# Hedgehog attention and maxout FFN on one core: q and k of all 16 units loaded as bf16 from GpSimd's queue, side by side in the transposed tile

## The chip, the cores and the metric

The kernel runs on one core of one Trainium2 chip. The metric is the device time of one execution in microseconds (us). A profile of one execution stands beside it. In its rows PE is TensorE, PEld its weight loads, DVE VectorE, ACT ScalarE, POOL GpSimd and SP SyncE; a q behind a name (POOLq, SPq) is that engine's sequencer, which issues transfers and waits on semaphores. L565 is line 565 of the kernel.

## The reference

```python
def phi(x):                                    # x: [8, 8, 576, 64]; w_phi: [64, 128]
    proj = np.einsum('bhsd,df->bhsf', x, w_phi)
    proj = proj - np.max(np.abs(proj), axis=-1, keepdims=True)
    return np.concatenate([np.exp(proj), np.exp(-proj)], axis=-1)
q_p, k_p = phi(q), phi(k)
kv  = np.einsum('bhsf,bhsd->bhfd', k_p, v)
z   = np.sum(k_p, axis=2)
num = np.einsum('bhsf,bhfd->bhsd', q_p, kv)
den = np.einsum('bhsf,bhf->bhs', q_p, z)[..., None] + 1e-06
x   = (num / den)                              # -> [4608 tokens, 512]
h   = np.maximum(np.maximum(x @ w1, x @ w2), x @ w3)   # w1, w2, w3: [512, 768]
out = h @ w_out                                        # w_out: [768, 512]
```

The row maximum of `phi` is taken out of the exponent: the kernel makes exp(p) and exp(-p) without it and puts the factors exp(-m) and exp(m) on v (for k) and on the quotient (for q).

## The kernel before, in words

**Units and chunks.** The attention is cut into 16 units of 4 heads, two units per batch element. A unit has 18 tiles of 128 rows of q and 18 of k: 16 main tiles of q (the first 512 positions of each head) and two tiles of "tails" (the last 64 positions of the four heads). The FFN is cut into nine chunks of 512 tokens: chunk b takes the main tokens of units 2b and 2b+1, the ninth the tails of all of them.

**A unit** runs through these steps (line numbers of the profile):

- Loads. Units 0 to 3 (`by_pe`) load q and k as bf16 into `qk_bf` by transfers that GpSimd issues (L450, L465), except that k of unit 0 comes as float32 by SP (L457) and is cast by DVE (L461). Units 4 to 15 load q and k as float32 into `q_raw` and `k_raw` by SP's queue, and GpSimd casts them into `qk_bf` in four or five pieces per unit (L509). The tails of q come by SP in two small transfers for two units. v comes by SP as float32 into `v_raw`; the loads of v of units 1, 2 and 3 wait for a one-element copy on DVE (`gate`, L478).
- Transposition to `qkT`. Units 0 to 3: TensorE transposes into the PSUM tile `tps` (L494), DVE copies out (L499). Units 4 to 15: one DMA transpose from SP's queue (L513). A tile of q lies above the k tile of the same number (rows 0 to 63 and 64 to 127 of one column block; the other way round from tile 8 on).
- Projections "G" (L535): for each tile one 64-row product for q (`psq`) and one for k (`psk`), in two halves of the array at a time. ACT makes exp(p) and exp(-p) of k (`Ek`, L544), DVE the absolute row maxima (`mk`, `mq`, L547).
- ACT makes the factors `em` (L557); GpSimd multiplies v with them (`vab`, L565) and appends the factors (L569). TensorE sums "K" (L586, `kvps`), 72 products per unit.
- The projections of q the other way round "M" (L606, `psm`), their exponentials `Eq` on ACT (L612), the products "N" with `kv_sb` (L637, `psn`), the sum, reciprocal and quotient (DVE L640 to L645, GpSimd L647 into `x_sb`), and the transposition into `xT` (TensorE and copies for units 0 to 5, a DMA transpose on SP for the rest).

**FFN.** max(x@w1, x@w2, x@w3) is computed from differences: w2 - w1 and w3 - w1 are formed in `w_bf` on GpSimd and DVE (L762), one matmul per difference follows (`ups`, L687), evacuated with a maximum (L693 to L697), and the part through w1 is put into the output as one product with w1@w_out. That product is made once, from a transposed w1 (L774) and w_out (L788). The output products are L715 and L720, the evacuation L728, the stores L735. The four weight loads are issued by GpSimd (L420). A chunk's products need `xT` of its two units and the differences.

**What sets the order.** Every step is a `Node`. The string `PLAN` lists all nodes in the order of their issue, with the engine (T is TensorE, D DVE, A ACT, G GpSimd, S SP), the numbers of the buffers, and after the @ a due time; the nodes are emitted in this order, and each engine works through its own share of it strictly in order, waiting at an instruction whose operand isn't ready. A transfer that GpSimd issues is an instruction in GpSimd's order like any other: its waits hold up what stands behind it. Transfers of one queue take turns on eight semaphores; the ninth issue on a queue waits until the first has landed, the tenth until the second, and so on.

Of the kernel before, what the change touches and what calls it, by code (L numbers as in the profile page):

```python
# [16 lines left out]
DF = 128  # L17
DM = H * D
# [12 lines left out]
GROUPS = [(0, 4), (4, 4), (8, 4), (12, 4), (16, 2)]  # L31
BATCHES = [(0, 8), (8, 8), (16, 2)]
# [7 lines left out]
JOIN = 2  # L40
MOVE = 5
VA_DVE = 1
QK = 3
# [41 lines left out]
8S0@0.7 5G0@1.2 6S@1.3 2S@1.9 4G@2.1 10S0@3.1 9D@3.5 11S0@4.4 7D@4.5 0G@5.0 3D@5.3 92G1@5.6 15T0@6.0 93G@6.4 16D0@6.7  # L85
177G2@7.3 29T000100@7.4 34T23@7.7 31A@7.9 33D@7.9 13T4@8.0 37D@8.5 30A@8.5 12G@8.9 14D@9.1 176G@9.2 36A@9.3 17T0@9.3
38D@9.7 24T45@9.9 35A@9.9 96G@10.0 19T67@10.1 18D@10.3 26A@10.4 178S0@10.4 32D@10.6 39T03@10.7 68T200@10.8 21A@10.9
42D@11.2 25A@11.4 43D@11.5 40A@11.8 22D@11.9 58T10@12.0 48A0@12.1 41A@12.3 27D@12.5 51G0@12.5 20A@12.6 99T3@13.0
28D@13.1 69A@13.1 44A@13.4 63T75@13.6 61A@13.6 23D@13.7 47G@13.7 97T4@13.9 1173G@13.9 65A@14.1 100D1@14.3 101T6@14.4
59A@14.5 50G@14.7 102D@14.9 70A@15.0 98D@15.1 118T013611@15.3 60A@15.3 94D@15.7 64A@15.8 46G@15.8 122D@15.8  # L90
152T411@15.9 95S@16.0 103T12@16.0 120A@16.3 106D@16.5 184T3@16.7 62A@16.8 49G@16.9 107D@17.1 182T7@17.1 104A@17.2
121D@17.7 154A@17.7 113T01@17.8 105A@18.0 45G@18.1 185D0@18.3 153A@18.5 71A0@18.8 183D@18.9 55T024@18.9 67A@19.0
252G1@19.2 114A@19.5 117D@19.5 52T37@19.7 56A@19.9 253G@20.0 57A@20.1 116D@20.1 66A@20.2 108T20@20.3 54A@20.7
112D@20.8 1176G@20.9 147T45@20.9 115A@20.9 111D@21.4 53A@21.4 123T72@21.5 119A@21.5 1174G@21.7 72T31@21.7 127D@22.0
125A@22.0 1187T6@22.2 151A@22.3 73D0@22.3 181G@22.5 126D@22.7 128A0@22.8 80T73@22.9 149A@23.0 74D@23.1 131G0@23.1
109A@23.5 1188D0@23.5 129G@23.5 1185T1@23.7 124A@24.0 81D1@24.1 148A@24.2 83T62@24.4 179D1@24.5 130G@24.6 82D@24.7
150A@24.7 186T7@24.8 1183T4@25.0 84D@25.1 110A@25.2 187D@25.5 75T53@25.6 132A@25.7 85D@25.8 1186A@25.9 133G@26.0
142T06@26.0 76D@26.2 136T072@26.3 86D0@26.6 1184D@26.8 143A@26.8 228T500@26.9 257T1@27.1 256G@27.2 137A@27.3 77D@27.4
87G0@27.4 138A@27.4 329S0@27.5 261T4@27.6 144A@27.6 206T007200@27.8 262D1@27.9 229A@28.1 210D@28.2 159T34@28.3
155A0@28.4 258D@28.5 230A@28.6 134G@28.6 156T07@28.7 400S@28.8 208A@28.8 90T5@29.0 78D0@29.1 146A@29.1 157D1@29.3  # L100
1193T1@29.3 327S@29.4 160D@29.7 135G@29.7 145A@29.8 1175G@29.9 328S0@30.0 158D@30.1 91A@30.2 161D@30.5 401S@30.7
197T3076@30.7 79G@30.7 1194A@30.9 209D@30.9 139T45@31.2 180S@31.3 162D1@31.3 198A@31.4 201D@31.4 1191T1@31.9
163G1@31.9 141A@32.0 200D@32.0 202A@32.2 140A@32.6 205D@32.7 207A@32.8 199A@33.1 167T34@33.2 1178G@33.2 204D@33.3
164T72@33.5 1192A@33.6 168D1@33.9 223T05@33.9 203A@34.1 259T1@34.2 165D@34.3 226A@34.5 169D@34.7 218T36@34.8 224A@35.0
88T7@35.1 166D@35.1 1195T4@35.4 227A@35.5 254D@35.5 170D1@35.7 255S@35.8 1179D@35.8 219A@36.0 89D@36.5 171G@36.5
221A@36.5 172T5@36.7 260D@36.9 220A@37.0 1189T27@37.0 225A@37.5 1D@37.5 1177D@37.7 222A@37.9 174T3@38.3 1181G@38.3
173D@38.3 1196A@38.4 188T6701@38.7 175D@38.9 1190A@38.9 293T4511@39.2 192D@39.4 1205T3@39.5 297A@39.6 190A@40.1
1201T6@40.4 1182D@40.4 193A@40.6 1180D@41.0 1206A0@41.1 1217T2@41.2 194A@41.6 191D@41.7 403G1@41.7 1202A@42.1
1213T3@42.1 405G@42.2 196D@42.3 331G2@42.5 294A@42.6 1218D@42.9 1207T6@43.0 404G@43.0 296A@43.1 1214D@43.5 189A@43.6
333G@43.6 1209T0@43.8 1208A@44.1 195D@44.1 332G@44.2 295A@44.6 281T117511@44.8 407G@44.9 272T1632@44.9 473S0@45.0  # L110
211A0@45.1 284D@45.2 1210A@45.3 1203T4@45.5 334G@45.5 543S@45.6 276D@45.6 277A@45.8 212G0@46.2 285D@46.2 475S@46.2
282A@46.3 1199T0@46.3 279D@46.6 1204A@46.6 283A@47.1 275D@47.2 1219T7@47.2 1200A@47.5 335S0@47.5 280D@47.8 278A@48.0
263T0154@48.2 213G@48.3 1220D@48.4 214A@48.4 274A@48.6 1211T2@48.7 270D@49.0 265A@49.1 273A@49.5 1215T7@49.6 266D@49.7
268A@50.0 267D@50.3 406G@50.4 286A1@50.5 215T063@50.6 231A0@50.7 1212D@50.9 269A@50.9 288G1@51.0 264A@51.4 1216D@51.5
303T2@51.8 298T40@51.9 216A@52.0 217D@52.1 1221T1@52.2 304A@52.3 271D@52.5 301A@52.6 287G@53.0 305A@53.1 240T36@53.1
544S0@53.3 1222D@53.3 302A@53.3 243T57@53.4 1231T2@53.7 289A@53.8 474S@53.9 241D1@53.9 299A@53.9 244D@54.4 408S1@54.5
300A@54.6 232T31@54.6 242D@54.8 235T50@54.9 306A1@55.1 477G0@55.1 245D@55.2 290T146@55.4 233D0@55.6 478G@55.7
236D@56.0 546G2@56.4 246D1@56.5 366T3700@56.6 292A@56.8 291D@56.8 1232T@56.9 547G@56.9 367A@57.1 237D@57.1 548G@57.5
234D@57.6 369A@57.6 247G1@57.8 368A@58.0 238D0@58.1 318T64@58.2 1233D0@58.4 370A@58.5 371T51@58.6 315T03@58.9
239G@59.0 374A@59.1 319D1@59.1 1223T2@59.2 316D@59.5 375A@59.7 320D@60.0 330S1@60.0 310T06@60.1 373A@60.2 479G@60.2  # L120
317D@60.4 248T1@60.4 476S0@60.7 307T47@60.8 549G@60.8 321D0@61.0 249A@61.0 1224T@61.1 311D0@61.1 683S0@61.3 322G0@61.3
308D@61.5 372A@61.6 613S@61.9 312D@61.9 309D@62.4 250T4@62.4 1225A1@62.6 409T11536111@62.8 313D1@62.9 251D@63.1
314G@63.2 439T7011@63.2 411A@63.5 413D@63.5 325T2@63.6 1227T4@63.9 415A@64.0 412D@64.1 1197G@64.4 440A@64.5 326D@64.7
323T5@64.7 443A@65.0 1228T@65.1 416D@65.2 410A@65.4 550G@65.5 324D@65.8 442A@65.9 417D@66.2 551S2@66.3 1247T5@66.4
441A@66.4 686G1@66.7 1229D2@66.8 414A@66.9 687G@67.3 336T00076300@67.3 1248A1@67.5 376T1@67.8 480G@67.9 427T24@67.9
344D@68.0 1235T5@68.1 377A@68.1 428A@68.4 431D@68.6 341A@68.7 339D@69.0 1236T@69.0 429A@69.2 342A@69.5 430D@69.6
337A@69.9 340D@70.0 615S@70.0 1243T4@70.3 378A@70.4 1237D3@70.6 338A@70.7 343D@71.2 345T2610@71.3 684S0@71.3
1244A@71.4 354T75@71.7 402S@71.9 1245T3@71.9 346A@72.0 352D@72.0 355A@72.5 614S@72.5 349D@72.6 347A@72.7 1255T4@72.8
688G@72.9 617G2@73.1 481S0@73.1 351A@73.2 348D@73.4 618G@73.7 1253T2@73.7 356A@73.7 353D@74.0 1246A@74.0 350A@74.5
1241T6@74.5 358D@74.6 690G@74.7 357D@74.9 1256D@75.3 1259T7@75.4 359A1@75.4 1242A@75.7 360G1@75.8 379A1@76.2  # L130
1254D@76.3 418T3450@76.4 1239T6@76.9 422D@77.1 423A@77.1 362A@77.6 421D@77.7 1251T1@77.8 361G@77.8 425D@78.3 419A@78.4
1261T3@78.7 1240D@78.9 420A@79.1 1260D@79.5 1249T2@79.5 424A@79.6 1234S@79.6 619G@79.9 432A0@80.0 426D@80.1 753S0@80.2
# [159 lines left out]
def kernel(  # L292
# [58 lines left out]

    raws = {}
    loaded = {}

    def raw_bufs(u):
        if u // 2 not in raws:
            raws[u // 2] = [buf(f"{x}_raw", 2 if x == "v" else 1, [P, 2 * UT, D], FP32) for x in "qkv"]
        return raws[u // 2]  # L360
# [494 lines left out]
```

## Time and profile before

| | |
|---|---|
| median of 3 runs | 291.16 us (290.9 to 291.44) |
| the profiled execution: its own time | 292.95 us |
| its span, from the first to the last instruction | 291.2 us |
| TensorE busy | 268.1 us, 92% of the span |
| DVE, ACT, GpSimd busy | 237.7, 190.7, 163.5 us |
| mean granted TensorE clock | 0.991 |
| read from HBM, written to HBM | 34.67 MB, 9.44 MB |

A row of the chain of waits in order of time has the start, the duration and what ran (or what was waited for). A row of the timeline has the start, the duration of the merged instructions, the engine, the line, the operation and the count, and in brackets the idle time before it with what ended that. A row of busy time by stretch has the stretch, its length, then for PE, PEld, DVE, ACT and POOL the busy time and the number of instructions, then the granted clock of TensorE, the share of the 16 DMA engines (it can exceed 1, since packets of two queues overlap on one engine) and GB/s.

### The profile page before, as it was taken

Reading aid. Unit: us, or ns where it says so; the run is one execution under the profiler, and the core shown is the slowest. Engines: PE = TensorE matmul, PEld = TensorE weight load, DVE = VectorE, ACT = ScalarE, POOL = GpSimd, SP = SyncE. Lnnn points to the kernel's source line nnn. Section 1 sums busy time; section 2 is a strip of 40 time slices with the busy share of each in tenths; the row PEclk is TensorE's granted clock in tenths of the full one; section 3 lists DMA queues with packets and bytes.
Section 4 is the critical chain, followed back from the end, with each engine's and each line's share of the span. In section 5 each row is a group of like instructions: output and inputs, shape, how many; then the busy total and the mean of one; then the engine's idle time right before and its main releaser. Section 6 shows DMA issues by size and latency. Waiting matters only on the chain.

```text
span 291.2 us, 8530 instructions
## 1 busy us (share of the span) xinstructions
PE 268.1 (92%) x3457; PEld 151.1 (52%) x3502; DVE 237.7 (82%) x474; ACT 190.7 (65%) x471; POOL 163.5 (56%) x169
## 2 busy tenths in 40 slices
PE   1898896998999899999999999998999999999993
PEld 1566552465546454664565455664454664444442
DVE  2889887898899789988999999988989895674641
ACT  1799894987986699589963899898969820000000
POOL 6297859798479787795495536855526373000000
PEclk9999997999999999999999999999999999999998
DMA  8989994999799999999997427993504105200054
GB/s 160 228 175 187 253 287 195 196 254 300 160 297 260 204 356 203 211 283 217 282 244 196 136 46 184 227 138 100 156 2 118 73 2 128 108 0 2 0 161 129
DMA packets 70664, 49.94 MB, mean 172 GB/s; under 512 B 47072, under 2 KB 58720, under 8 KB 70624
## 3 DMA queue, kind: packets, MB, share of 16 engines
q1 hardware_dynamic: 65232, 44.25, 61.8%
q0 software_dynamic: 5312, 5.08, 11.1%
q8 instruction: 27, 0.44, 0.6%
q14 instruction: 13, 0.11, 0.1%
q10 hardware_dynamic: 80, 0.07, 0.1%
HBM read 34.67 MB, written 9.44 MB: 151 GB/s over the span
## 4 chain that ended last, share of the span: by engine, by line
PE 74%; DMA 10%; POOL 4%; issue 4%; ACT 4%; DVE 3%; POOLq 0%; DVEq 0%
PE ups L687 31%; PE ops L720 13%; PE ops L715 9%; PE kvps L586 6%; PE psn L637 5%; DMA w_bf<-in_moe_w_dram 5%; PE psq L535 5%; PE psm L606 3%; ACT Ek L544 2%; DMA xT<-x_sb 2%; POOL w_bf L762 2%; DMA qk_bf<-in_q_dram 2%; PE tps L494 2%; POOL vab L565 1%; POOL x_sb L647 1%
## 5 line engine op out<-in xcount | busy, mean ns | idle before, releaser
L687 PE MATMUL ups<-xT,w_bf 128*128 128x512 bf16 x410 | 100.4, 384 | 4.8 <-POOL w_bf L762 2.6
L544 ACT ACTIVATE Ek<-psk 128x512 bf16<-128x512 f32 (+1 forms) x160 | 84.2, 576 | 16.3 <-PE psk L535 11.9
L612 ACT ACTIVATE Eq<-psm 128x512 bf16<-128x512 f32 (+1 forms) x160 | 82.7, 583 | 12.7 <-PE psm L606 10.8
L565 POOL TENSOR_TENSOR vab<-v_raw,em 128x1152 bf16<-128x1152 f32 (+1 forms) x36 | 67.8, 1907 | 22.6 <-ACT em L557 19.9
L687 PEld LDWEIGHTS <-w_bf 128*128 128x128 bf16 x432 | 40.1, 99 | 52.5 <-issue 5.6
L547 DVE TENSOR_REDUCE mk<-psk 128x4 f32<-128x512 f32 (+1 forms) x80 | 49.5, 630 | 4.8 <-PE psk L535 3.6
L647 POOL TENSOR_TENSOR x_sb<-y,rden 128x640 bf16<-128x640 f32 x32 | 40.4, 1270 | 19.0 <-DVE rden L645 12.1
L720 PE MATMUL ops<-wout_bf,hT 128*128 128x512 bf16 (+1 forms) x214 | 50.0, 373 | 0.7 <-issue 0.5
L547 DVE TENSOR_REDUCE mq<-psq 128x4 f32<-128x512 f32 (+1 forms) x80 | 48.4, 627 | 2.1 <-PE psk L535 2.1
L693 DVE TENSOR_TENSOR hT<-hT,ups 128x512 bf16<-128x512 bf16 x54 | 36.2, 678 | 8.1 <-PE ups L687 7.2
L728 ACT COPY osb<-ops 128x512 f32<-128x512 f32 (+1 forms) x11 | 6.4, 578 | 53.9 <-PE ops L720 53.9
L640 DVE TENSOR_TENSOR y<-psn,sq 128x325 f32<-128x325 f32 x64 | 29.3, 487 | 4.2 <-PE psn L637 4.1
L720 PEld LDWEIGHTS <-hT 128*128 128x128 bf16 x222 | 20.6, 98 | 22.5 <-issue 1.1
L643 DVE TENSOR_TENSOR y<-y,psn 128x325 f32<-128x325 f32 x64 | 29.6, 486 | 1.2
L637 PEld LDWEIGHTS <-Eq 128*128 128x128 bf16 x640 | 24.8, 97 | 9.5 <-issue 2.4
L637 PE MATMUL psn<-kv_sb,Eq 128*128 128x65 bf16 x640 | 26.9, 194 | 1.2 <-issue 1.0
L728 DVE COPY osb<-ops 128x512 f32<-128x512 f32 (+1 forms) x26 | 17.5, 677 | 12.7 <-PE ops L720 11.8
L535 PE MATMUL psq<-wph,qkT 64*128 64x128 bf16 x288 | 25.0, 225 | 1.4 <-DVE qkT L499 1.2
L535 PEld LDWEIGHTS <-qkT 64*128 64x128 bf16 x576 | 18.5, 97 | 14.2 <-issue 10.3
L535 PE MATMUL psk<-wph,qkT 64*128 64x128 bf16 x288 | 24.5, 225 | 0.3 <-DVE qkT L499 0.2
L715 PE MATMUL ops<-xT 128*128 128x512 bf16 x86 | 24.0, 380 | 0.7 <-issue 0.2
L586 PE MATMUL kvps<-vab,Ek 64*128 64x65 bf16 x1152 | 22.3, 191 | 1.5 <-issue 1.1
(57 smaller groups left out, 260.8 us busy)
## 6 DMA issues: line engine op xcount, KB each, us to landing
v_raw<-in_v_dram SPq DMA_DIRECT2D x16, 576.0 KB, 5.9
out_dram<-osb SPq DMA_DIRECT2D x32, 256.0 KB, 3.0
k_raw<-in_k_dram SPq DMA_DIRECT2D x12, 576.0 KB, 5.6
q_raw<-in_q_dram SPq DMA_DIRECT2D x12, 512.0 KB, 6.1
w_bf<-in_moe_w_dram POOLq DMA_DIRECT2D x3, 768.0 KB, 12.5
q_raw<-in_q_dram SPq DMA_DIRECT2D x16, 64.0 KB, 5.5
qk_bf<-in_k_dram POOLq DMA_DIRECT2D x3, 288.0 KB, 8.0
qk_bf<-in_q_dram POOLq DMA_DIRECT2D x3, 256.0 KB, 5.7
```

The costliest lines, as they stand in the source:

```text
L535: nc.tensor.matmul(ps()[:, i, :], lhsT=cols[r0:r0 + D, :], rhs=wph[r0:r0 + D, :], start=True, stop=True)
L544: "ek", {"ACT": 0.485 if n == 4 else 0.28}, lambda s=s, t0=t0, n=n, psk=psk: nc.scalar.activation(Ek[s]()[:, t0:t0 + n, :], psk()[:, 0:n, ...
L547: reds.append(nd(kind, {"DVE": 0.607 if n == 4 else 0.34}, lambda ps=ps, m=m, t0=t0, n=n: nc.vector.tensor_reduce(m()[:, t0:t0 + n], ps()[ ...
L565: made.append(any_of(n_, lambda n_, g=g, t0=t0, t1=t1: (nc.vector if n_.eng == "DVE" else nc.gpsimd).tensor_tensor(vab()[:, g, t0:t1, 0:D] ...
L586: nc.tensor.matmul(kvps[ab]()[:, pr, g, :], lhsT=Ek[g]()[r, t, :], rhs=vab()[r, g, t, :], start=(pr == prs[0] and g + j == 0), stop=(pr == ...
L612: "eq", {"ACT": 0.485 if n == 4 else 0.28}, lambda s=s, t0=t0, n=n, psm=psm: nc.scalar.activation(Eq[s]()[:, t0 * P:(t0 + n) * P], psm()[: ...
L637: nc.tensor.matmul(psn[g]()[:, c, :], lhsT=Eq[g]()[:, t0:t0 + P], rhs=kv()[:, pr, ab, g, :], start=True, stop=True)
L647: divs.append([any_of(n_, lambda n_, pr=pr, y=y, rden=rden: (nc.vector if n_.eng == "DVE" else nc.gpsimd).tensor_tensor(x_sb()[:, pr].rear ...
L687: nc.tensor.matmul(ups(), lhsT=w_bf[i + 1][:, ct, j * P:(j + 1) * P], rhs=tokens_of(ct), start=(ct == 0), stop=(ct == CT - 1))
L693: nc.vector.tensor_tensor(hT()[:, j, :], hT()[:, j, :], ups(), ALU.max)
L715: nc.tensor.matmul(ops_()[:, 0:width], lhsT=tile_of(ct, tt), rhs=line_w[c_i > MOVE][:, ct, cols], start=(ct == 0), stop=False)
L720: nc.tensor.matmul(ops_()[:, 0:width], lhsT=hT()[:, j, tt * P:(tt + 1) * P], rhs=wout_bf[:, j, cols], start=False, stop=(j == JT - 1))
```

## The change

1. q and k of all units are loaded as bf16 straight into `qk_bf` by transfers that GpSimd issues (k of unit 0 stays as it was). The tiles `q_raw`, `k_raw` (but for unit 0) and the 54 casts of L509 are gone; the tails of q go through a small tile `q_tail` and one cast per unit (16 in all, 12 on GpSimd, 4 on DVE). `qk_bf` has five buffers in place of three.
2. In `qkT` two neighbouring tiles of q lie in one column block, one above the other (9 blocks), and then 9 blocks of k. Units 0 to 3: one transposition makes a full 128x128 block, 18 per unit in place of 36.
3. The projections of q and of k are separate nodes (four nodes of eight 64-row products each), and the two tiles of tails have one node of six products (`pst`) that also holds the product of the "M" kind for them. A unit has 5 nodes "G" (before: 3, and 5 in units 0 and 1) and 2 nodes "M" (before: 3).
4. `PLAN` is new throughout. GpSimd makes the identity ahead of its first load; its first instructions are then, in the built program (each number of a load counts GpSimd's transfers):

```
identity; load 1, 2: q of unit 0; 3: q of unit 1; 4: k of 1; 5: k of 2; 6: w1; 7: q of 2; 8: w_out
tail cast of unit 0; of unit 1
load 9: k of 3 (waits for load 1); 10: w2 (waits for 2); 11: k of 4 (3); 12: q of 3 (4); 13: k of 5 (5, and for the buffer of unit 0)
load 14: w3 (waits for load 6, w1); 15: q of 4 (waits for load 7, q of 2); 16: q of 5 (waits for load 8, w_out)
tail casts of units 3 and 2
unit 0: vab factors, vab x3, factors, vab
unit 1: factors, vab x3; load 17: k of 7; x_sb of unit 0; factors, vab of unit 1; x_sb of unit 0; x_sb of unit 1
difference w2 x2; x_sb of unit 1; difference w2; vab of unit 2, factors, vab; tail cast; difference w3; vab of unit 3 x2 ...
```

In the order before, GpSimd's loads are q of 0 (two), q of 1, k of 1, k of 2, q of 2, w1, then the four vab of unit 0, then q of 3, k of 3, w_out, w2, and w3 among the work of units 0 and 1.

The diff, cut to its core:

```diff
-QK = 3
+QK = 5
-        qk = buf("qk_bf", QK, [P, 2, UT, D] if by_pe else [P, UT, 2 * D], BF16)
-        qkT = un["qkT"] = buf("qkT", 3, [P, UT * P], BF16)
+        qk = buf("qk_bf", QK, [P, 2, UT, D], BF16)
+        qkT = un["qkT"] = buf("qkT", 3, [P, UT, P], BF16)
...
-        else:
-            main_q.append(nd("L", {"SP": 0.62}, lambda: load(u, 0, nc.sync, 0), [], [qb], ...))
-            main_k.append(nd("L", {"SP": 0.62}, lambda: load(u, 1, nc.sync, 0), [], [kb], ...))
+            def load_k():
+                nc.gpsimd.dma_start(qk()[:, 1, :, :].rearrange("p (r j) d -> p r (j d)", j=PT), rows_of(1, u, 0, 2))
...
-            pieces = [(0, 0, 8), (0, 8, last)] + [(0, MT, UT)] * (u % 2) + [(1, 0, 8), (1, 8, UT)]
-            for c, t0, t1 in pieces:
-                n_ = nd("C", {"POOL": 0.13 + 0.055 * (t1 - t0)}, None, need, [(qb, kb)[c], qk])
...
-                            nc.tensor.transpose(tps()[r:r + D, n, :], qk()[:, c, t0 + n, :], ident)
+                            nc.tensor.transpose(tps()[:, n, :], qk()[:, c, 2 * m:2 * m + 2, :].rearrange("p a d -> p (a d)"), ident)
...
+        for h in range(2):
+            for c in (1, 0):
+                pss = [bank("psk" if c else "psq", [P, HB, DF]) for _ in range(2)]
+                def proj(h=h, c=c, pss=pss):
+                    for i in range(HB):
+                        for par in range(2):
+                            r = slice(par * D, par * D + D)
+                            nc.tensor.matmul(pss[par]()[:, i, :], lhsT=qkT()[r, block(c, h * HB + i), :], rhs=wph[r, :], start=True, stop=True)
...
+        def ends(pss=pss):
+            for i in range(3):
+                for par in range(2):
+                    r = slice(par * D, par * D + D)
+                    cols = qkT()[r, block(i % 2, 8), :]
+                    a_, b_ = (wph[r, :], cols) if i == 2 else (cols, wph[r, :])
+                    nc.tensor.matmul(pss[par]()[:, i, :], lhsT=a_, rhs=b_, start=True, stop=True)
```

More of the change, by code (lines that the diff above doesn't have):

```diff
@@ L30 @@
 PT = UT // 2
[L31 to L32 removed]
+HB = MT // 4
 XW = SM + P
@@ L349, with tail_buf, value_buf @@
     copy_on = {"DVE": nc.vector.tensor_copy, "ACT": nc.scalar.copy, "POOL": nc.gpsimd.tensor_copy}
-    raws = {}
+    tails, vals = {}, {}
     loaded = {}
[L357 to L360, printed above, removed]
+    def tail_buf(u):
+        if u // 2 not in tails:
+            tails[u // 2] = buf("q_tail", 2, [P, 4, D], FP32)
+        return tails[u // 2]
+    def value_buf(u):
+        if u // 2 not in vals:
+            vals[u // 2] = buf("v_raw", 2, [P, 2 * UT, D], FP32)
+        return vals[u // 2]
     def rows_of(what, u, p0, p1):
@@ new lines, in attention @@
+        if u % 2 == 0:
+            loaded[0] = nd("Lt", {"SP": 1.25}, lambda: load_tail(u), [], [qb], pipe=0.96, lat=1.7, dmas=2, packet=30.0)
+        gates = []
+        if u < len(GATES) and GATES[u]:
+            src = units[GATES[u][0]]["qkT"]
+            gates.append(nd("gate", {"DVE": 0.1}, lambda src=src: nc.vector.tensor_copy(
+                v_part(u, 0, 1)[0:1, 0, 0:1], src()[0:1, block(1, 0), 0:1]), units[GATES[u][0]]["Tc"][0:1], [src, vb]))
+        main_v = nd("Lv", {"SP": 0.62}, lambda: load_v(u), gates, [vb], pipe=1.6, hold=-3.0, lat=1.7, packet=100.0)
@@ L607, in mm @@
                                      start=True, stop=True)
[L608 to L609 removed]
+            need = list({id(x): x for x in (there[0, h * HB + i] for i in range(HB))}.values())
+            a = nd("M", {"PE": 0.225}, mm, need + [n_phi], [qkT] + psms + Eq, mode=1)
+            for par in range(2):
+                c0 = (8 * h + 4 * par) * P
```

582 lines of the change are left out of this document (287 added, 295 removed).

## The prediction

> **What bounds the kernel now.** I read the page's sums first, then busy time by stretch, then the chain of waits in order of time. The stretches are cut where the chain turns: at 20.51 us (the first K), 42.41 (the first product of the FFN) and 62.66 (the K of unit 3); the last two rows are a close-up.
>
> ```profile
> span 291.2 us, 8530 instructions
> ```
> ```profile
> 0.00:20.51 20.51, 12.57 (x171) 8.74 (x172) 12.93 (x25) 11.96 (x28) 11.88 (x22) 1.00 0.96 177
> 20.51:42.41 21.90, 19.84 (x388) 13.74 (x392) 20.07 (x49) 20.77 (x56) 16.18 (x18) 1.00 1.15 240
> 42.41:62.66 20.25, 17.30 (x206) 8.81 (x209) 16.69 (x27) 15.86 (x42) 16.70 (x15) 0.92 0.83 222
> 62.66:240.00 177.34, 171.81 (x2469) 97.69 (x2505) 160.86 (x333) 141.70 (x346) 115.07 (x112) 1.00 0.79 184
> 44.00:48.00 4.00, 1.38 (x5) 0.42 (x5) 3.80 (x4) 2.61 (x6) 3.75 (x3) 0.90 0.81 316
> 48.00:52.00 4.00, 3.78 (x13) 1.45 (x12) 2.60 (x5) 1.18 (x3) 3.80 (x7) 0.67 0.03 9
> ```
> ```profile
> 22.31 14.25 DMA w_bf<-in_moe_w_dram
> 36.63 2.12 POOL w_bf L762
> 38.76 1.66 POOL x_sb L647
> 40.42 3.79 issue
> 44.25 2.63 POOL w_bf L762
> 46.93 1.21 PE ups L687 x3
> ...
> 62.66 1.26 PE kvps L586 x72
> ```
>
> Two regimes. From 62.66 on TensorE is the bound: 171.8 of 177.3 us busy, 5.5 us idle in all, and there a change is worth what it takes from TensorE. Ahead of that the kernel waits for weights and for GpSimd: w2 lands at 36.6, its difference and the last `x_sb` of unit 1 end near 40.4, products start at 42.41, and at 44.25 the difference for w3 is still missing, which leaves TensorE idle until 46.93 and then at half clock for a while (0.90 and 0.67 in the close-up). So I price three stages: A up to the first product (42.41), B up to the K of unit 3 (20.25 us), C the rest (291.2 - 62.66 = 228.5 us).
>
> **Stage A: a wait that GpSimd gets.** GpSimd's rows of before, and two of TensorE:
>
> ```profile
> 1.24 1.61 POOL L450 DMA_DIRECT2D qk_bf<-in_q_dram  x2 [0.80 <-POOLq L839]
> 2.85 0.22 POOL masks.py:197 MEMSET ident<- 128x128 bf16 x1
> 3.15 0.29 POOL masks.py:199 TENSOR_SCALAR_AFFINE_SELECT ident<-ident 128x128 bf16<-128x128 bf16 x1
> ...
> 9.46 0.28 POOL L486 CAST qk_bf<-q_raw 128x128 bf16<-128x128 f32 x1 [3.90 <-DMA q_raw<-in_q_dram]
> ...
> 14.64 0.26 POOL L569 CAST vab<-em 128x18 bf16<-128x18 f32 x1 [0.97 <-ACT em L557]
> 14.79 0.74 POOL L420 DMA_DIRECT2D w_bf<-in_moe_w_dram  x1
> 15.54 4.48 POOL L565 TENSOR_TENSOR vab<-v_raw,em 128x576 bf16<-128x576 f32 x4
> ...
> 32.50 2.48 POOL L647 TENSOR_TENSOR x_sb<-y,rden 128x640 bf16<-128x640 f32 x2
> ```
> ```profile
> 32.28 1.47 PE L788 MATMUL pm<-wout_bf,hT 128*128 128x512 bf16 x5 [0.89 <-DMA wout_bf<-in_moe_w_out_dram]
> ```
> ```profile
> q1 hardware_dynamic: 65232, 44.25, 61.8%
> q0 software_dynamic: 5312, 5.08, 11.1%
> ```
>
> In before the four `vab` of unit 0 start at 15.54. In the changed order all sixteen first loads stand ahead of them on GpSimd, and the sixteenth (q of unit 5) waits until the eighth (w_out) has landed, since it needs the same semaphore. GpSimd works in order (at 9.46 it sat 3.90 us before one cast while a load stood ready behind it), so unit 0's `vab`, its K, and everything that TensorE, DVE and ACT have ordered behind that K wait until w_out is in. Call that moment X.
>
> X, first way: GpSimd's queue (q0) moved 5.08 MB in 11.1% of the span, 32.3 us of all 16 engines, 6.4 us per MB. Up to w_out the new order has 2.95 MB in it (q 256 KB three times, k 288 twice, w1 and w_out 768 each): 18.7 us. SP's queue moved 44.25 MB in 180 us, 4.1 us per MB; k of unit 0, w_phi, two pairs of tails and v of units 0 and 1 are 2.1 MB: 8.5 us. Together 27.2 us at a share of 1; at the shares of the two first stretches, 0.96 and 1.15, 23.7 to 28.3, from 1.8 us on (1.24 plus the identity's 0.5, which now comes first): 25.5 to 30. Second way: in before w_out is there at 32.28; what it then stood behind and no longer does is q and k of unit 3 (0.56 MB, 3.5 us), and w1 was only issued at 14.79, when 1.38 MB (8.8 us) had been queued since 1.24, so the queue stood empty for up to 2 us: 27 to 29. If SP's transfers hide wholly, 1.8 + 18.7 = 20.5 would be the floor. I take X = 27.
>
> From X, GpSimd's own chain: the sixteenth load 0.8, two tail casts 0.6, factors 0.26 and two `vab` at 1.12 each: the first K of unit 0 can start at X + 3.9 = 31, against 20.51. Then the other six `vab` of units 0 and 1 (6.7), factors three times (0.8), one load (0.7), four `x_sb` at 1.24 (5.0), two differences at 2.12 (4.2): X + 21.3, and about 0.5 for a reciprocal that comes late. From the end of that last `x_sb` to the first product before took 2.0 us (40.42 to 42.41): X + 23.8. TensorE has been idle for ten us by then and starts slow (the close-up shows half clock after a shorter gap); its own chain and DVE's (20.1 of 21.9 us busy) have little slack, so I add 0.4: **the first product at X + 24.2 = 51.2, +8.8 us**. Below X + 22.5 or above X + 26 I have no reason to go.
>
> The Trainium skill speaks against this change twice here. "DMA: Bandwidth & Descriptors" (section Anatomy of one DMA) says that DMA engines do not wait on semaphores and that the wait happens on the issuing sequencer: the trace's 3.90 us at 9.46 agrees, as far as one row can. "TensorE: Matmul & The Clock Gate" (Part 1) gives about 3.4 us idle until half rate and as long until full rate; the trace's gap before 46.93 was 2.6 us and still cost clock. By that page the restart costs 1.7 to 3.4 us on TensorE in place of my 0.4, and the sum would be 1 to 3 us more.
>
> **Stage B** gives back. The weights come earlier (w3 is the fourteenth load, behind w_out by 2.7 MB or 17 us at 6.4 us per MB, so at about X + 17 = 44, ahead of the first product), so the idle time until 46.93 (2.6 us) goes, and with it the half clock (0.10 and 0.33 of 4 us each, 1.7). What is late next is then only the chain of stage A. Two projection groups and one M pair of unit 3 have moved ahead of the first product: 0.23 each, 0.7. **20.25 becomes 15.25: -5.0 us.** Bounds: -3 if DVE, ACT and GpSimd (16 of 20 us busy each) lag by what TensorE gains, -5.7 if all of TensorE's 20.25 - 17.30 goes.
>
> **Stage C.** Rows for what is removed and for a change of form on TensorE (chain; a projection group between products):
>
> ```profile
> L509 POOL CAST qk_bf<-q_raw 128x512 bf16<-128x512 f32 (+2 forms) x30 | 16.9, 586 | 7.9 <-DMA q_raw<-in_q_dram 7.2 <-DMA qkT<-qk_bf 0.5
> L509 POOL CAST qk_bf<-k_raw 128x512 bf16<-128x512 f32 (+1 forms) x24 | 15.8, 666 | 4.8 <-DMA k_raw<-in_k_dram 4.8
> ...
> L494 PE MATMUL tps<-ident,qk_bf 128*64 128x128 bf16 x144 | 8.4, 287 | 6.3 <-DMA qk_bf<-in_q_dram 6.0 <-ACT Ek L544 0.3
> ```
> ```profile
> 79.47 0.16 PE psq L535
> 79.63 0.05 PE psq L535
> ...
> 80.13 0.32 PE ups L687
> 80.45 0.05 issue
> 80.50 4.05 PE ups L687 x18
> ```
>
> - GpSimd loses 54 casts (32.7 us) and gets 24 more load issues (0.74 each, 17.8) and 8 more tail casts (0.28, 2.2): -12.7 us on an engine that is 65% busy here. Worth something only where TensorE waits for it; I cost it at nothing by itself.
> - Transfers: q and k of 12 units leave SP's queue (13.4 MB, 55 us of engine time at its rate) for GpSimd's (6.7 MB landed, 43 us). With a share of 0.79 neither counts: nothing, bounds -1 and +2 us (transposes of `qk_bf` that come late).
> - TensorE: the first product after a projection group takes 0.32 instead of 4.05/18 = 0.225, with a pause of 0.05, and the group's first pair 0.16 instead of 0.05: 0.26 us per insertion. After the K of unit 3 the order of before has 39 such insertions, the new one 34: -1.3. The tails' two pairs and one M product become three pairs, about 0.04 per unit, 12 units: -0.5.
> - Of the 5.5 us idle some goes with the earlier q and k: -0.8, bounds 0 and -2.5.
> - The halved transpositions (8.4 us to 4.2) lie in stage A, before the wait for X, which hides them; without that wait they would be worth up to what TensorE lacks there, about 2 us. The sums, maxima and exponentials keep count and size (8 of 512 columns and 2 of 256 for each kind); four tail casts come to DVE, 0.8 us, beside other work.
>
> **C: -2.6 us** (bounds -4.5 and +1). Sum on the span: 8.8 - 5.0 - 2.6 = +1.2, that is 292.4. The profiled span (291.2) and the median of the runs (291.16) agree, the profiled execution's own time is 1.8 above both; I carry the difference over to the median: 291.2 + 1.2 = **292.4 us**.
>
> **Rivals.**
> 1. *w_out lands early (the other side).* One place, the wait of the sixteenth load; each us of X is a us of the sum. Even with before at X = 25.8, under 290.6 for X < 25.2. For it: SP's and GpSimd's transfers overlap (share 1.15). Against it: both ways above give 25.5 or more. At X = 22 the time is 287.4. The Trainium skill's fit for a transfer from GpSimd ("DMA: Bandwidth & Descriptors", Anatomy of one DMA: 2.0 us and 436 GB/s) gives, with source bytes, about 22 for X; the one weight load of the page, 14.25 us from issue to landing at 22.31, shows that here it doesn't hold beside other traffic.
> 2. *The start isn't caught up.* ACT and DVE are 95 and 92% busy in the second stretch; shifted by ten us, with the slow clock, they may start the first product at X + 26 and B may give only -3.5: 8.8 + 1.8 - 3.5 - 2.6 = +4.5, 295.7.
> 3. *GpSimd's order hurts later too.* Each of the 24 new issues can hold GpSimd until an earlier transfer or the transpose that frees its buffer has landed. Two such waits of 2 us in C that reach TensorE, without the gains of C: 8.8 - 5.0 + 2.5 = +6.3, 297.5.
> 4. *The change does nothing that counts* (C 0, the wait at X as forecast): +3.8, 295.0; I put it with 2.
>
> **How the numbers follow.** Forecast with X from 25.5 to 29: 0.43; rival 1 0.27; rivals 2 and 4 0.20; rival 3 0.10. Within 0.2% is 290.6 to 291.7, about what a measurement of this kernel can tell from no change. Rival 1 gives 0.25 faster and 0.02 same, the forecast 0.05 faster, 0.12 same and 0.26 slower, the others 0.30 slower: faster 0.30, same 0.14, slower 0.56. Range: from X = 23 (288.4) to beyond rival 2: 288.4 to 296.5; the forecast's own range is 290.5 to 294.5.
>
> **What would show it.** In the changed profile GpSimd should sit idle for some ten us in all ahead of the issues of w3 and of q of units 4 and 5, the last time until w_out lands, and the first `vab` of unit 0 should start at 26 to 31, the first K near 31 and the first product near 51, with TensorE at half clock after 30. After it there should be no wait for the difference of w3. If the first `vab` starts near 16, the step with the semaphore is wrong; if the first product is near 45, X or the chain behind it was too long; if stage C isn't shorter than 228.5 by one to four us, the insertions and idle time were misread.

## The result, and the profile after

The changed kernel is slower: the ratio of its time to that of before is **1.0073, 95% interval 1.0044 to 1.0103**. Its median is 293.40 us over 20 runs; 293.4 / 1.0073 puts before at 291.3, so the change costs 2.1 us. The ratios of this document are of fast executions, those within 1.5% of the fastest of their kernel: here ten of before's 20 and one of the changed kernel's 20 are left out (over all of them the medians are 293.89 and 293.40, so the sign hangs on this choice), and in experiment 2 one of 1491 us. The forecast was 292.4 us, 1.2 more than before, with 0.56 for slower: the direction was right, the size 0.9 us short. One caution for all that follows: the profiled execution of before, at 293.0 us, lay 1.7 us above that 291.3, that of the changed kernel (293.4, span 291.6) at its median. The stages of the two profiles therefore differ by 0.4 us in all, not by 2.1; experiment 6 says where the 1.7 may lie.

From the page of the changed kernel:

```profile
span 291.6 us, 8376 instructions
...
q1 hardware_dynamic: 55632, 30.88, 43.7%
q0 software_dynamic: 14912, 11.77, 28.1%
```

SP's queue (q1) lost 13.4 MB and GpSimd's (q0) gained 6.7, as forecast. Busy time by stretch, cut at the first K (28.50), the first product (48.80) and the K of unit 3 (65.36; stage C follows below):

```profile
0.00:28.50 28.50, 13.81 (x128) 8.42 (x129) 15.23 (x31) 18.96 (x42) 14.99 (x29) 1.00 1.10 211
28.50:48.80 20.30, 19.68 (x375) 14.52 (x378) 17.66 (x45) 16.85 (x45) 19.16 (x18) 1.00 0.95 173
48.80:65.36 16.56, 15.00 (x189) 8.24 (x191) 16.27 (x29) 12.83 (x31) 11.97 (x9) 1.00 0.48 107
```

| stage | before | forecast | after |
|---|---|---|---|
| A, to the first product | 42.41 | 51.2 (+8.8) | 48.80 (+6.4) |
| B, to the K of unit 3 | 20.25 | 15.25 (-5.0) | 16.56 (-3.7) |
| C, the rest | 228.5 | 225.9 (-2.6) | 226.2 (-2.3) |
| sum | | +1.2 | +0.4 |

Stage A is the wait that the prediction is about. GpSimd's timeline, with the idle time ahead of a row in brackets:

```profile
18.54 0.76 POOL L419 DMA_DIRECT2D w_bf<-in_moe_w_dram  x1 [3.84 <-DMA w_bf<-in_moe_w_dram]
20.71 0.74 POOL L446 DMA_DIRECT2D qk_bf<-in_q_dram  x1 [1.42 <-DMA qk_bf<-in_q_dram]
25.94 0.74 POOL L446 DMA_DIRECT2D qk_bf<-in_q_dram  x1 [4.48 <-DMA wout_bf<-in_moe_w_out_dram]
26.67 0.53 POOL L474 CAST qk_bf<-q_tail 128x128 bf16<-128x128 f32 x2
27.14 0.26 POOL L600 CAST vab<-em 128x18 bf16<-128x18 f32 x1
27.30 3.37 POOL L596 TENSOR_TENSOR vab<-v_raw,em 128x576 bf16<-128x576 f32 x3
...
46.34 1.25 POOL L679 TENSOR_TENSOR x_sb<-y,rden 128x640 bf16<-128x640 f32 x1
...
54.18 2.11 POOL L794 TENSOR_TENSOR w_bf<-w_bf 128x1024 bf16<-128x1024 bf16 x1
```

Three loads wait for the load eight places earlier: 9.7 us of idle time in all, "some ten" in the forecast. The last one ends when w_out is in: X = 25.94. TensorE meanwhile, with a later row of the same sums for comparison:

```profile
28.50 0.57 PE L617 MATMUL kvps<-vab,Ek 64*128 64x65 bf16 x14 [8.18 <-POOL vab L596]
...
30.23 2.38 PE L806 MATMUL pwT<-ident,w_bf 128*128 128x128 bf16 x24
...
41.25 0.39 PE L617 MATMUL kvps<-vab,Ek 64*128 64x65 bf16 x14
...
48.80 1.90 PE L719 MATMUL ups<-xT,w_bf 128*128 128x512 bf16 x8
```

It is idle 8.18 us and comes out slow: 14 sums take 0.57 us at 28.50 and 0.39 at 41.25. Once the second `vab` is there it waits for nothing more: the chain of waits runs on TensorE from 29.62 to the first product.

```profile
29.62 0.68 PE kvps L617 x18
30.30 2.31 PE pwT L806 x24
...
47.35 0.75 PE pxT L689 x10
48.10 0.60 PE psq L542 x16
```

Stage B, the chain of waits, and the forms row of the differences (durations min/median/max in ns, first and last start):

```profile
52.38 0.68 DVE hT L729
53.26 0.60 DVE hT L729
53.85 3.59 DVE w_bf L794 x2
57.58 0.35 DVE kv_sb L623
57.97 0.38 PE ups L719
```
```profile
L794 DVE TENSOR_TENSOR w_bf<-w_bf x2: 677/1875/3073, 53.8 to 56.8; 128x1024 bf16<-128x1024 bf16 x2
```

The wait for GpSimd's difference of w3 that before has at 46.93 is gone, but a shorter one has come on DVE: of two equal differences one takes 3.07 us and one 0.68. The slow one runs while GpSimd makes its own difference (54.18 to 56.29 above). Stage C has a wait that before doesn't have:

```profile
138.83 1.08 ACT Eq L528 x2
140.14 8.88 DMA v_raw<-in_v_dram
149.18 4.21 POOL vab L596 x2
153.43 1.33 PE kvps L617 x72
```

SP issues the load of v of unit 9 at 140.14, behind the transposes in its order; it lands 8.9 us later, GpSimd's `vab` wait for it, and TensorE is idle 1.69 us ahead of 153.43. The whole of stage C, before and after:

```profile
62.66:291.20 228.54, 218.37 (x2699) 119.82 (x2738) 188.04 (x376) 142.07 (x347) 118.76 (x116) 1.00 0.67 160
65.36:291.60 226.24, 216.63 (x2718) 120.27 (x2750) 180.63 (x362) 148.62 (x364) 109.51 (x99) 1.00 0.68 141
```

TensorE's busy time fell by 1.7 us, its idle time by 0.6 (10.2 to 9.6), GpSimd's busy time by 9.3. Some records of TensorE are missing from both traces, so both idle times are too long; their difference is good to a few tenths.

### The profile page after: what moved, and what is told of

It is laid out like the page before. It is cut to its first block, busy times and chain, and to the rows that moved or that the text cites. A ratio compares the mean times of both kernels' runs of the same rounds, so it can differ in the third digit from the quotient of the medians.

```text
span 291.6 us, 8376 instructions
## 1 busy us (share of the span) xinstructions
PE 265.1 (91%) x3405; PEld 151.4 (52%) x3446; DVE 229.8 (79%) x464; ACT 197.3 (68%) x481; POOL 155.6 (53%) x153
## 4 chain that ended last, share of the span: by engine, by line
PE 75%; DMA 9%; DVE 5%; POOL 5%; issue 3%; ACT 1%; SPq 0%; POOLq 0%; DVEq 0%
PE ups L719 25%; PE ops L752 16%; PE ops L747 10%; PE psn L669 7%; PE kvps L617 6%; DMA qk_bf<-in_q_dram 5%; DMA v_raw<-in_v_dram 3%; PE psk L542 2%; PE psm L637 2%; POOL vab L596 2%; DVE m L531 2%; PE psq L542 2%; PE pm L820 2%; POOL qk_bf L446 1%; DVE w_bf L794 1%
## 5 line engine op out<-in xcount | busy, mean ns | idle before, releaser
L528 ACT ACTIVATE Ek<-psk 128x512 bf16<-128x512 f32 x128 | 72.2, 628 | 7.7 <-PE psk L542 7.0
L528 ACT ACTIVATE Eq<-psm 128x512 bf16<-128x512 f32 x128 | 72.7, 625 | 2.3 <-PE psm L637 2.2
L531 DVE TENSOR_REDUCE m<-psk 128x4 f32<-128x512 f32 x64 | 42.2, 681 | 1.4 <-ACT Ek L528 0.8
L531 DVE TENSOR_REDUCE m<-psq 128x4 f32<-128x512 f32 x64 | 41.9, 679 | 1.6 <-PE psq L542 1.4
L727 ACT ACTIVATE hT<-ups 128x512 bf16<-128x512 f32 x32 | 19.2, 618 | 23.6 <-PE ups L719 23.3
L760 ACT COPY osb<-ops 128x512 f32<-128x512 f32 (+1 forms) x17 | 10.0, 588 | 33.7 <-PE ops L752 18.9
L528 ACT ACTIVATE Et<-pst 128x256 bf16<-128x256 f32 x64 | 24.8, 418 | 1.9 <-DVE m L531 0.9
L617 PEld LDWEIGHTS <-Ek 64*128 64x128 bf16 x1024 | 19.4, 95 | 12.5 <-issue 10.3
L669 PE MATMUL psn<-kv_sb,Eq 128*128 128x65 bf16 x512 | 24.8, 194 | 0.0
L760 DVE COPY osb<-ops 128x512 f32<-128x512 f32 (+1 forms) x20 | 13.5, 674 | 14.3 <-PE ops L752 12.5
```

Source lines behind the costliest of these rows:

```text
L528: nc.scalar.activation(out, ps, EXP, scale=1.0 - 2.0 * s)
L531: nc.vector.tensor_reduce(out, ps, AXX, ALU.max, apply_absolute_value=True)
L617: nc.tensor.matmul(kvps[ab]()[:, pr, g, :], lhsT=Ek[g]()[r, t, :] if t < MT else Et[g]()[r, 0, t - MT, :], rhs=vab()[r, g, t, :], start=(p ...
L669: nc.tensor.matmul(psn[g]()[:, c, :], lhsT=Eq[g]()[:, t0:t0 + P] if c < 4 else Et[g]()[:, 1, pr, :], rhs=kv()[:, pr, ab, g, :], start=True ...
```

## The experiments

The theory: the wait of the sixteenth load for the eighth sets the start, one us of X is one us of the end, and stages B and C give part of it back by themselves. The rivals: weights or transfers bind the start in any case; the gain of C comes from GpSimd or the transfers, which the prediction costed at nothing. All but one were timed in five rounds against before. In PLAN words, 256 is the load of k of unit 3, 1150, 1148 and 1149 those of w_out, w2 and w3, 178, 331 and 402 those of q of units 2, 4 and 5, 1155 a difference for w3, 677 the load of v of unit 9.

**1. Which load is waited for.** Three kernels that only change GpSimd's order.

```diff
-1150G@7.1 256G3@9.1
+256G3@6.9 1150G@7.1
```

> The changed kernel with two neighbours swapped in GpSimd's order: k of unit 3 (the ninth load) now goes ahead of w_out (the eighth), nothing else. Theory (the sixteenth load waits for the eighth, and each us of that wait is a us of the end): the sixteenth load now waits for 0.29 MB instead of 0.77 MB and is issued near 22 instead of 25.94, the first K of unit 0 comes at about 24.6 instead of 28.50, and the time falls by 3.5 to 4 us, to about 289.5 (ratio to before about 0.995). Rival (the start is bound by the landing of the weights, the wait only fills a gap that is there anyway): the first product stays near 48.8 and the time within 0.5 us of the changed kernel's 293.4.

```diff
-1149G@12.9 331G@13.7 402G@14.5
+1149G@21.5 331G@21.8 402G@24.7
```

> The changed kernel with its last three early loads moved on GpSimd: w3 and q of unit 4 behind the vab of unit 0, q of unit 5 behind three of the vab of unit 1. Theory: GpSimd's three waits (3.8, 1.4 and 4.5 us) leave the path, the vab of unit 0 start near 15.5, the first K near 17, the first product near 39 to 40 instead of 48.80, and the time falls by 8 to 9 us, to about 285 (ratio to before 0.977). Rival 1 (weights bind the start): w_out at 26 and the difference for w2 hold the first product at 42.4, where before has it, or later; time 287 or more. Rival 2: w3, issued some 3 us later, is missing after the first products as it was in before, which gives 2 to 4 us back: 287 to 289.

```diff
-178G@6.3 1148G@9.9
+1148G@7.3 178G@9.95
```

> The changed kernel with w2 ahead of q of unit 2 in GpSimd's order: w_out becomes the seventh load and w2 the eighth, so that the fifteenth load waits for w_out and the sixteenth for w2. Theory: 0.5 MB more stand ahead of the load that is waited for, at 6.4 us per MB the sixteenth issue goes from 25.94 to about 29.2 and the time rises by 3.3 us, to about 296.7 (ratio 1.018). Rival (weights bind the start): w2 is there 1.7 us earlier, so the time stays or falls by up to 1.7 us.

GpSimd's timeline with k of unit 3 ahead of w_out (the lines of these three kernels and of the next are numbered 3 lower):

```profile
23.08 0.74 POOL L443 DMA_DIRECT2D qk_bf<-in_q_dram  x1 [0.96 <-DMA qk_bf<-in_k_dram]
```

With w2 among the first eight:

```profile
24.39 0.74 POOL L443 DMA_DIRECT2D qk_bf<-in_q_dram  x1 [4.03 <-DMA wout_bf<-in_moe_w_out_dram]
28.79 0.74 POOL L443 DMA_DIRECT2D qk_bf<-in_q_dram  x1 [3.65 <-DMA w_bf<-in_moe_w_dram]
```

With the three loads behind the `vab`:

```profile
17.73 0.26 POOL L597 CAST vab<-em 128x18 bf16<-128x18 f32 x1 [2.22 <-ACT em L585]
18.50 3.37 POOL L593 TENSOR_TENSOR vab<-v_raw,em 128x576 bf16<-128x576 f32 x3 [0.51 <-DMA v_raw<-in_v_dram]
```

| kernel | X | first K | first product | K of unit 3 | span | ratio to before (95%) |
|---|---|---|---|---|---|---|
| three loads behind | none | 21.49 | 42.04 | 58.5 | 284.6 | 0.9775 (0.9726 to 0.9824) |
| k of 3 ahead of w_out | 23.08 | 25.66 | 46.32 | 62.7 | 288.6 | 0.9967 (0.9936 to 0.9999) |
| changed kernel | 25.94 | 28.50 | 48.80 | 65.4 | 291.6 | 1.0073 (1.0044 to 1.0103) |
| w2 among the first eight | 28.79 | 31.36 | 52.60 | 69.0 | 295.3 | 1.0181 (1.0137 to 1.0225) |

The wait moves to whichever load stands eighth (k, w_out, w2 in the brackets), and the time follows: 2.86 us of X between the second row and the third are 1.06% or 3.1 us, 2.85 us between the third and the fourth 1.08%. (The second and the fourth were timed against the same runs of before: 5.71 us of X, 2.14%, 6.2 us.) The rival that weights bind the start falls, also where w2 came earlier. In the first row GpSimd waits for ACT's factors and v instead, so the first K is at 21.5 and not at 17, the first product at 42.04 and not at 39 to 40 as expected, yet the ratio was met. That 42.04 lies near the 42.4 which the weights rival gave, but no weight stands on its chain: from 9.6 on that runs on TensorE, DVE and ACT, and GpSimd's difference for w2 starts at 35.41 without a wait. Without the wait the changed kernel is 2.2% faster than before.

**2. The wait of stage B.** GpSimd's last difference for w3 goes to DVE.

```diff
-1155G@45.4
+1155D@45.15
```

> The changed kernel with GpSimd's last difference for w3 (2.1 us at 54.18) given to DVE, so that DVE makes all three of the late ones. Theory on stage B: the first of DVE's two differences takes 3.07 us there and the second 0.68, since the first runs beside GpSimd's; alone each takes about 0.65, so three take 2.0 instead of 3.67, the wait of TensorE's weight load and product at 57.97 (1.3 and 1.4 us) goes, and the time falls by about 1.4 us, to 292.0. Rival: DVE is the bound there in any case, or the products then wait for something else; no change within 0.4 us.

Measured: 1.0112 (1.0058 to 1.0167), no gain that shows. By stretch and by form:

```profile
50.21:65.30 15.09, 15.09 (x192) 8.16 (x190) 14.62 (x29) 12.66 (x31) 9.89 (x8) 1.00 0.47 106
```
```profile
L791 DVE TENSOR_TENSOR w_bf<-w_bf x3: 679/679/981, 55.2 to 56.7; 128x1024 bf16<-128x1024 bf16 x3
```

Stage B does what was expected: three differences in 0.68 + 0.68 + 0.98 = 2.3 us instead of two in 3.07 + 0.68 = 3.75, and 15.09 us in place of 16.56. But X was 27.05 in this execution, which takes 1.1 back, and stage C took 229.2 instead of 226.2: the same v of unit 9 landed at 149.7, TensorE was idle 2.52 us ahead of that K and came out at a lower clock (0.96 from 140 to 180). The longer idle time is 0.8 of the 3.0 us; TensorE's busy time in stage C, 220.8 us, is 1.2 longer than in the kernel with k of 3 ahead of w_out (219.7), whose trace has as many records. The rest wasn't followed up. So the next two kernels issue that v early, with and without the moved difference; the second is the pair of both edits.

```diff
-677S@129.3
+677S@106.3
```

> The changed kernel with the load of v of unit 9 issued on SP right behind that of unit 8 (due 106.3 in place of 129.3). Theory (the idle time in stage C counts one to one, and the wait of GpSimd for that v, 5.43 us at 149.18, which leaves TensorE idle 1.69 us at 153.43, is a new one): first vab of unit 9 near 144, the idle time at 153 gone, time 1.7 us less than the changed kernel's 293.4 (ratio to before about 1.001). Rival (something else is late next there, K of the next unit or the exponentials): less than 0.5 us.

> The changed kernel with GpSimd's last difference for w3 given to DVE and with the early v of unit 9. Theory (giving the difference to DVE gains 1.4 us ahead of the K of unit 3, and these were lost again at the wait for the v of unit 9, whose load SP issues at a time of its own): both gains stand, 1.4 + 1.7 = 3.1 us, time about 290.3, ratio to before 0.997. Rival (the difference on DVE costs elsewhere what it gains): as with the early v alone, about 1.001, or worse.

With the early v alone, by stretch, and GpSimd at unit 9:

```profile
49.20:65.80 16.60, 15.04 (x192) 8.28 (x194) 16.31 (x29) 12.82 (x31) 11.98 (x9) 1.00 0.50 108
```
```profile
146.45 4.20 POOL L596 TENSOR_TENSOR vab<-v_raw,em 128x1152 bf16<-128x1152 f32 x2 [2.41 <-ACT em L588]
```

With both:

```profile
48.85:64.00 15.15, 14.99 (x193) 8.21 (x196) 14.68 (x29) 12.66 (x31) 9.89 (x8) 1.00 0.51 110
```

Measured: 1.0021 (0.9980 to 1.0062) and 0.9974 (0.9939 to 1.0008), against 1.001 and 0.997 expected. In the first, stage C takes 290.8 - 65.8 = 225.0 us, 1.2 less than in the changed kernel's profile; in the second, stage B is 15.15. By the profiles both gains stand when both edits are made. The runs show less. The early v alone isn't shown by them: its median is 293.29 us against the changed kernel's 293.40, and the lower ratio was taken against other runs of before. The interval of both edits (up to 1.0008) does lie below the changed kernel's (from 1.0044). What the late v costs also changes from one execution to the next: with its load at the old place the idle time ahead of that K was 0.48, 0.56 and 0.71 us in the three kernels of experiment 1.

**3. All three edits together.**

> All three moves: w3, q of units 4 and 5 behind vab of units 0 and 1, GpSimd's last difference for w3 on DVE, v of unit 9 early. Theory (the gains are in separate stages and add): with the late loads alone 285.1; TensorE's idle time there is 1.25 us at 51.06 and 0.56 us at 145.8, so 283.3, ratio to before 0.971. Rival (the start is then bound by something else): 285, ratio 0.977.

Measured: 283.91 us, **0.968 (0.963 to 0.973)**, span 282.7: the fastest here, 3.2% faster than before. It is below the moved loads alone (0.9775), though the two intervals just meet (0.9726 and 0.973).

**4. GpSimd's time in stage C.** A cast that nobody needs behind each load of q and k from unit 4 on, then from unit 6 on with the early v:

```diff
+    def more(u):
+        if u >= 4:
+            nc.gpsimd.tensor_copy(extra, wphi_f.unsqueeze(1).to_broadcast([P, 4, DF]))
```

> The changed kernel with a cast of 128x512 f32 added on GpSimd behind each of the 24 loads of q and k of units 4 to 15; its result goes to a tile that nobody reads. That puts about 24 x 0.6 = 14.4 us of busy time back on GpSimd, mostly in stage C, where the change took 12.7 away. Theory (GpSimd's busy time in stage C counts nothing): within 0.5 us of the changed kernel, ratio to before 1.007. Rival (stage C is shorter because GpSimd is lighter): 2 us or more longer, ratio 1.014 or more.

> The changed kernel with the early v of unit 9 and with a cast of 128x512 f32 added on GpSimd behind each of the 20 loads of q and k of units 6 to 15 (20 x 0.62 = 12.4 us, the size of what the change took from GpSimd; none of them ahead of the vab of unit 0), results read by nobody. The 24 casts of the kernel with the late v of unit 9 cost 3.7 us in stage C, and most of it came at that v. Theory (GpSimd's time counts only where its work holds up SP's order ahead of that v): stage C as with the early v alone, 225.0, the sum within 0.7 us of it, ratio to before 1.000 to 1.005. Rival (GpSimd's busy time in stage C counts in itself, some 0.25 us per us): stage C 228 or more, ratio 1.011 or more.

The first measured 1.0166 (1.0092 to 1.0241): the theory falls. Some of it isn't stage C (four casts stand ahead of the first K, which came at 29.7, and a fifth in stage A), but stage C took 296.7 - 66.8 = 229.9, 3.7 us more. The second measured 1.0081 (1.0053 to 1.0109), between the two expectations. Its chain:

```profile
121.57 0.62 POOL extra L410
122.19 2.08 POOL vab L604
...
129.79 0.62 POOL extra L410
130.41 1.22 POOL x_sb L687
131.66 0.51 DVE y L680
132.21 0.87 PE psn L677 x20
```

Both kernels have 19 casts in stage C, 11.8 us. In the second, stage C takes 293.0 - 66.0 = 227.0 us, 2.0 more than with the early v alone, 0.17 us per us of cast. The runs give 1.7 us by the ratios (0.6%), which were taken against different runs of before, and 0.85 by the medians (294.14 and 293.29), so 0.07 to 0.17 us per us. GpSimd is on the chain from before 118 to 131 with five of the casts, 3.0 us. That only casts on such a chain cost something fits this, but wasn't tried. Where the other 1.7 of the first kernel's 3.7 us come from isn't shown either: its idle time ahead of the K of unit 9 is 2.49 us, 0.8 longer than the changed kernel's.

**5. TensorE's slow restart.** 24 products of the identity ahead of the first K:

```diff
+    for _ in range(24):
+        todo.append((19.05, make(3, True)))
...
+        src = ident if early else idle
```

> The changed kernel with 24 products of the identity with itself (128x512, result read by nobody) on TensorE ahead of the first K of unit 0, so that TensorE isn't idle from 20.3 to 28.5 and comes out of GpSimd's wait at full speed. In the changed kernel the 24 transpositions of w1 at 30.23 take 2.38 us, 107 ns each, against 56 ns for transpositions later in the run. Theory (GpSimd's chain sets the first product, TensorE's slow restart is hidden): the transpositions take half as long, the time stays within 0.6 us of the changed kernel, ratio to before 1.005 to 1.008. Rival (the restart costs TensorE 1.7 us or more, and this is in the sum): 1.7 us less, ratio 1.001.

```profile
21.22 15.31 PE L859 MATMUL idler<-ident 128*128 128x512 bf16 x24 [0.17 <-ACT Et L530]
36.59 0.57 PE L619 MATMUL kvps<-vab,Ek 64*128 64x65 bf16 x14
...
37.69 2.15 PE L808 MATMUL pwT<-ident,w_bf 128*128 128x128 bf16 x24
```

This didn't test what it was made for. The products took 0.64 us each, until 36.53, 8 us past the moment at which the first K could have started, and TensorE was as slow behind them as after the idle time (0.57 and 2.15). The time went to 1.0267 (1.0204 to 1.0330). What it does show is that the first K itself carries the start: 8.1 us later there, 7.3 at the first product (56.08). And TensorE waits for nothing between the two: its own work from the first K to the first product takes 19.5 us, of the 20.3 in the changed kernel. What the slow restart costs in the changed kernel stays open.

**6. Before, profiled once more.**

> The kernel before, profiled a second time. Its first profile has a granted clock of 0.92 in the stretch from the first product to the K of unit 3 (0.67 from 48 to 52) and 0.98 after 240. Theory A (that is the idle time of 2.62 us at 46.93, so it belongs to the kernel): the same dip at the same place, first product near 42.4, K of unit 3 near 62.7, rest 228.5. Theory B (it belongs to that execution): no dip, 18.5 us in place of 20.25 for that stretch, and 227.5 for the rest.

```profile
48.00:52.00 4.00, 3.95 (x12) 1.45 (x12) 3.03 (x5) 0.77 (x2) 4.00 (x8) 0.57 0.08 30
```
```profile
47.46 5.31 PE L687 MATMUL ups<-xT,w_bf 128*128 128x512 bf16 x15 [3.31 <-POOL w_bf L762]
```

The wait for w3 and the half clock behind it come again at the same place, with 42.25 for the first product, 20.9 us for stage B and 229.4 for stage C. But this execution took 294.3 us, and both profiled ones have a mean granted clock of 0.991. Among the 66 timed executions of before in these comparisons, the 25 with a clock of 0.996 or more have a median of 291.3 us, the 19 below 0.992 one of 294.6. As far as that clock can be trusted (last section), the 291.3 that the ratio compares with is mostly made of executions that spent less time at half clock. How much of the wait and of the half clock they have isn't shown, and the 1.7 us between the profile of before and 291.3 may lie there. The prediction counted 1.7 us of half clock as something that stage B of before always pays.

**7. More transfers.** The load of q of units 4 to 15 issued twice:

```diff
+                if u >= 4:
+                    nc.gpsimd.dma_start(
+                        extra[:, t0:t1, :].rearrange("p (h j) d -> p h (j d)", j=SM // P),
+                        q[b, h0 + t0 // 4:h0 + t1 // 4, 0:SM, :].rearrange("h (p j) d -> p h (j d)", p=P))
```

> The changed kernel with the load of q of units 4 to 15 issued twice on GpSimd's queue, the second time into a tile that nobody reads: 12 more issues (9 us of GpSimd) and 3.1 MB more landed, 12 x 1.7 = 20 us of all DMA engines by before's 6.4 us per MB. Theory (transfers in stage C are hidden): within 0.6 us of the changed kernel, ratio 1.007. Rival (stage C is shorter because less is transferred there, or GpSimd's issues hold up the vab): 2 us or more longer, ratio 1.014 or more.

```profile
POOL extra L452 <- DMA extra<-in_q_dram: 25.3, 4, 13.8
```

Measured: 1.0978 (1.0912 to 1.1045). It says little on transfers: the twelve loads share one tile, each waits on GpSimd until the one before has landed (25.3 us in four waits, the longest 13.8), and the first K went to 44.80. It is the mechanism of stage A once more, larger. That transfers in stage C are hidden wasn't shown.

## Why the prediction came out as it did

- **X, right.** 25.94 against 27 (25.5 to 30), and between 25.61 and 27.05 in six further executions in which the same load is waited for. That the sixteenth load waits for the eighth is shown by moving other loads into that place. The 3.90 us at 9.46 that the prediction calls in for it is the wait of a cast; the three rows of stage A (3.84, 1.42 and 4.48 us) show it for issues. The estimate from the Trainium skill ("DMA: Bandwidth & Descriptors", Anatomy of one DMA: 2.0 us and 436 GB/s), about 22, was 4 us too early beside other traffic.
- **The chain from X to the first product, 1.3 us too long, and from the second `vab` on not GpSimd's.** The first K came at X + 2.56, not X + 3.9, because it starts behind the first `vab`, not the second. From there the prediction follows GpSimd, but the chain of the profile follows TensorE, which waits for nothing from 29.62 on and alone needs 19.5 us (experiment 5). GpSimd's sum fits all the same: the last `x_sb` of unit 1 ended at 47.59, X + 21.65 against X + 21.8 forecast. Both engines are nearly full from the first K to the first product (19.7 and 19.2 of 20.3 us), and that a sum along GpSimd comes out right is in part luck. From the end of that `x_sb` to the first product it took 1.2 us, not 2.0. The slow restart, 0.4 in the sum, stands on TensorE's chain: 24 transpositions took 2.31 us, and at the 0.056 each of later ones (10 in 0.56 at 44.25) it would be 1.35, so by this estimate 1.0 us was lost on these alone. The Trainium skill ("TensorE: Matmul & The Clock Gate", Part 1) asks for more than 0.4; the trace has the slow stretch (0.57 against 0.39). How much earlier the first product would be without it, with GpSimd as full, no run shows.
- **Stage B, mechanism right, size off.** "There should be no wait for the difference of w3" was wrong by one: GpSimd's wait went, and DVE's difference of 3.07 us took its place. With it moved, stage B is 15.09 and 15.15, and 15.25 had been forecast. The 1.7 us of half clock in the -5.0 is a reading of the profile of before; the executions that the ratio compares with may have less of it (experiment 6).
- **Stage C, sum right, one part wrong.** TensorE's part came about as forecast: 1.7 us less busy time for 1.8 (insertions 1.3, tails 0.5, not separated). Idle time fell by 0.6 for 0.8, but as the difference of two things. The late v of unit 9, which no step foresaw, took 1.69 us of idle time in this execution, so elsewhere 2.2 us of it went. The step that failed is GpSimd's 12.7 us, "I cost it at nothing by itself". In stage C its busy time fell by 9.3 us; at the measured 0.07 to 0.17 us per us this is worth 0.7 to 1.6 (an estimate, since the added casts don't stand where the removed ones stood). That the sum still came out is in part luck: the saving that was left out and the late v pull in opposite directions.
- **The rivals.** Rival 1 (w_out early) has the right slope, 1.1 us of time per us of X; between the runs at 23.08 and 25.94 its break-even lies at X = 24.0 by the ratios, not 25.8, about the 1.7 us by which the profile of before was long. Rival 2 (start not caught up) half came: B gave 3.7, but the first product was early. Rival 3 (GpSimd's order in stage C) came in another form, SP's order, at 140; its sum has 2.5 where the two waits of 2 us that it names make 4.0 (299.0, not 297.5). Rival 4 (nothing gained in C) didn't come by the profiles: C gave 2.3.
- **The sum.** Errors of -2.4 (A), +1.3 (B) and +0.3 (C) leave the profiles 0.8 below the forecast. That the runs lie 0.9 above it comes from the profiled execution of before, on whose span the sum was made. The two have opposite signs, so part of the closeness of 292.4 to 293.4 is luck.

## What to carry to other kernels

A load that is moved ahead isn't free on the engine that issues it: count which earlier transfer its issue must wait for, and put work that the path needs ahead of any issue that can wait. Here three loads moved behind the work that they held up turn a 0.7% loss into a 2.2% gain. An engine that is 60% busy can still be on the chain in places, so a saving on it should be priced from the chain, not from its share.

## What the runs showed of the hardware

- A difference on DVE (both inputs in SBUF) took 0.68 us alone and 3.07 beside one on GpSimd. In before the longest of four took 2.6, also beside GpSimd's (44.25 to 46.87):

```profile
L762 DVE TENSOR_TENSOR w_bf<-w_bf x4: 624/712/2605, 38.6 to 44.8; 128x1024 bf16<-128x1024 bf16 x4
```

The Trainium skill ("SBUF — State Buffer", Who interferes with whom) says that such an operation contends with GpSimd's reads, and that the order of issue decides which of the two is held up. The changed kernel's trace agrees that they hold each other up: GpSimd's takes its usual 2.11 us there, and DVE's ends 0.55 us after it, about as if it had run behind it, though in the rows DVE's starts first (53.77 against 54.18). In before both lose time: GpSimd's takes 2.62 us beside the 2.6 of DVE's. The kernel that gives all three to DVE has 0.68 as their median.
- The granted clock of a profile can miss a slow stretch. The kernel with the early v shows 0.50 where the changed kernel, with the same durations, shows 1.00:

```profile
28.20:32.20 4.00, 3.56 (x58) 3.33 (x58) 1.55 (x4) 0.56 (x5) 3.59 (x6) 0.50 1.27 204
```
```profile
28.19 0.57 PE L617 MATMUL kvps<-vab,Ek 64*128 64x65 bf16 x14 [7.62 <-POOL vab L596]
```

The durations of equal instructions are the safer sign.
